# First k cast, V and W1 casts, and the order of batch 1's loads in a fused attention and MLP kernel

## The chip, the cores and the metric

The kernel runs on one core of one Trainium2 chip. The metric is the time on the device in microseconds, lower is better. The core's engines run side by side and meet at semaphores: TensorE (PE) multiplies matrices and transposes, VectorE (DVE), ScalarE (ACT) and GpSimd (POOL) work element by element, and SyncE (SP) issues most of the transfers (DMAs).

## The reference

Eight batches of 576 tokens with 8 heads of 64. Attention sees a window of 64 tokens; its output goes through a normalisation and a two-layer MLP with a residual.

```python
scores = scale * np.matmul(q, k.transpose(0, 1, 3, 2))
mask = (rel >= 0) & (rel < window)                       # window = 64
attn = softmax(np.where(mask, scores, -1000000000.0))
x = np.matmul(attn, v)                                   # heads side by side: [8, 576, 512]
xn = (x - mu) / np.sqrt(var + 1e-06) * g_ln
out = x + np.maximum(xn @ w_ch1, 0.0) @ w_ch2            # [512, 2048], [2048, 512]
```

## The kernel before

Inputs and weights are float32 in memory and are cast to float16 on the chip. The work is cut into nine groups: group b (0 to 7) is the first 512 tokens of batch b, and group 8 the last 64 tokens of all batches. A group has four blocks of 128 tokens. One block goes through these steps:

- `t_main` (from L268) transposes q or k of half a group on TensorE and copies the result from PSUM to `qkT`. Groups 0 to 2 use it.
- `s_mm` (L302) multiplies k by q and lets ScalarE take the exponential into `pt`; `s_mask` multiplies by the mask on VectorE. In group 0 the mask is added on TensorE.
- `b_step` (L369) multiplies `pt` by V. It needs V twice: in `vA` as it is, and in `vB` shifted by 64 tokens. For group 0 and half of group 1, `vB_cur` and `vB_prev` (L194, L197) fill `vB` from the float32 V, on the engine that is given by a number: 0 is ScalarE, 1 is VectorE. VectorE then divides by the sums (L387, L390) and takes mean and variance (L392, L394).
- `z_step` (L406) normalises to `z`, `zt_step` (L447) transposes `z` to `zT`.

The MLP of a group follows: the first layer (L512, and L549 for half a group at a time) multiplies `w1g` by `zT` and ScalarE takes the maximum with zero (L516, L554); the second layer multiplies the result `hrT` by `w2s`. In group 0 the second layer is `l2_three` (L557), whose matmuls are at L563: three blocks of tokens side by side, staggered by one step, so that the step (i, 0) is the first that reads W2 tile i, which is 256 rows of W2. The last block of tokens follows in `l2` (L525). From group 2 on the second layer is a scheme of seven products (L590).

W1 comes in eight tiles (`w1_load`, i = 0 to 7): column quarter i // 2, and rows i % 2. The first four lie in a pool of four buffers, the last four in the memory that `w2s` takes later. `w1_cast(i, c, engine, lo, hi)` (L232) scales by the normalisation's gain and casts half of a tile's rows. W2 comes in eight tiles through the same pool of four buffers (`w2_load`, L242), so that tile i + 4 can only be loaded once GpSimd has cast tile i (`w2_cast`, L249).

The order of the work is written by hand. The instructions of an engine run in the order in which the program names them. What comes ahead of the loop is a list of calls (from L647). In the loop each group's matmuls are cut into units, and `at(u, f, ...)` puts the call f behind unit u. SyncE's queue is the order of the load calls: q, k and v of batch 0, the eight tiles of W1, q and k of the first half of batch 1 (`load_qk(1, 0)`), and the first four tiles of W2. The rest stands in `rest_of_loads` (L731), which is called behind unit 7 of group 0 and gives both SyncE's and GpSimd's order for batch 1. `keep_clock` issues matmuls whose result isn't used.

Of the kernel before, what the change touches and what calls it, by code (L numbers as in the profile page):

```python
# [11 lines left out]
FP16 = mybir.dt.float16  # L12
# [6 lines left out]
def kernel(  # L19
# [10 lines left out]
    nc = tc.nc  # L30
# [118 lines left out]
    def cast_q(b, x, half, act=False):  # L149
        t = qk32.pop((b, x, half))  # L150
        dst = p_in.tile([128, 8, 2, D], FP16, tag=f"qk16_{x}", name=f"qk16_{x}_{b}_{half}")
        qk16[(b, x, half)] = dst
        j = 8 if b < NPE else 2 if x == 1 else 4
        cp(act, dst[:, :].rearrange("p (a j) e d -> p a e j d", j=j),
           t[:, :].rearrange("p (a e j d) -> p a e j d", e=2, j=j, d=D))

    def alloc_v(b):
        vA[b] = p_va.tile([128, 4, H, D + 1], FP16, tag="vA", name=f"vA_{b}")
        nc.gpsimd.memset(vA[b][:, :, :, D:D + 1], 1.0)
# [18 lines left out]
    def cast_v(b, c0, c1, act=False):  # L178
        cp(act, vA[b][:, c0:c1, :, 0:D], v32[b][:, c0:c1])
# [9 lines left out]
    def init_vB(b):  # L189
        alloc_vB(b)  # L190
        nc.gpsimd.memset(vB[b][:, :, :, D:D + 1], 1.0)
        nc.gpsimd.memset(vB[b][0:64, 0, :, D:D + 1], 0.0)
# [59 lines left out]
    def alloc_qkT(b):  # L252
        qkT[b] = [p_qkt.tile([128, NHP, SM + 64 * x], FP16, tag=f"qkT{x}", name=f"qkT{x}_{b}") for x in range(2)]
        if b >= NPE:
            nc.gpsimd.memset(k_runs(b)[:, :, 0:32], 0.0)
        else:
            nc.gpsimd.memset(qkT[b][1][:, :, 0:64], 0.0)
# [4 lines left out]
    def evac(x, out, in_):  # L262
        if x == 0:
            nc.scalar.copy(out=out, in_=in_)
        else:
            nc.vector.tensor_copy(out=out, in_=in_)

# [397 lines left out]
    )  # L665
    nc.vector.tensor_scalar(out=mbias, in0=mask, scalar1=-1.0, scalar2=30000.0, op0=ALU.add, op1=ALU.mult)
    alloc_qkT(0)
    cast_q(0, 0, 0)
    alloc_v(0)
    cast_q(0, 1, 0)  # L670
    init_vB(0)
    cast_v(0, 0, 1)
    cast_v(0, 1, 2)
    cast_qk(0, 1)
    cast_v(0, 2, 3)
    cast_v(0, 3, 4)
    w1_cast(0, 0, nc.gpsimd)
    w1_cast(1, 0, nc.gpsimd, 0, 256)
    w1_cast(1, 0, nc.gpsimd, 256, 512)
    for i, lo in ((2, 0), (3, 0), (2, 256)):  # L680
        w1_cast(i, 0, nc.gpsimd, lo, lo + 256)

    for f in (alloc_qkT, alloc_v, init_vB):
        f(1)

    def keep_clock(n, pool=ps_t, tag="tp"):
        warm = pool.tile([128, 512], FP32, tag=tag, name="warm")
# [6 lines left out]
    keep_clock(9, ps_mm, "mm")  # L694
    t_main(0, 0, 0, 0)
    keep_clock(1, ps_mm, "mm")
    t_main(0, 1, 0, 1)
    keep_clock(1, ps_mm, "mm")
    vB_cur(0, 0, 0)
    vB_cur(0, 1, 0)  # L700
    vB_prev(0, 0, 1)
    vB_prev(0, 1, 1)
    s_mm(0, 0, True)
    s_mm(0, 1, True, (ps_mm, "mm"))
# [8 lines left out]
    vB_cur(0, 2, 0)  # L713
    keep_clock(2, ps_mm, "mm")
    s_mm(0, 2, True)
    vB_cur(0, 3, 1)
    vB_prev(0, 2, 1)
    keep_clock(1)
    zt_step(0, 1)
    w1_cast(0, 1, nc.scalar)  # L720
    b_step(0, 2)
    z_step(0, 2)
    w1_cast(1, 1, nc.scalar)
# [3 lines left out]
    load_qk(1, 0)  # L727
    for i in range(4):
        w2_load(i)

    def rest_of_loads():  # L731
        cast_qk(1, 0)
        for i in range(8):
            w2_cast(i)
            if i < 4:
                w2_load(i + 4)
        load_v(1, 0, 2)
        cast_v(1, 0, 1)
        cast_v(1, 1, 2)
        load_qk(1, 1)  # L740
        load_v(1, 2, 4)
        cast_qk(1, 1)
        cast_v(1, 2, 3)
        cast_v(1, 3, 4)
        load_qk(2, 0)
        load_qk(2, 1)

    def tail_casts(i, act, *us):
        return tuple((u, cast_tail, i, part, act) for part, u in enumerate(us))
# [12 lines left out]
    for g in range(NGRP):  # L762
# [33 lines left out]
        if g == 0:  # L796
            at(0, b_step, 0, 3)
            at(0, z_step, 0, 3)
            at(0, w1_cast, 2, 1, nc.scalar)
            at(0, w1_cast, 3, 1, nc.scalar)  # L800
            at(0, w1_cast, 3, 0, nc.scalar, 256, 512)
            at(1, zt_step, 0, 2)
            at(2, zt_step, 0, 3)
            for j in range(4):
                at(3 + j, w1_cast, 4 + j, 0, nc.vector)
                at(3 + j, w1_cast, 4 + j, 1, nc.gpsimd if j % 2 else nc.scalar)
                at(10 + j, r_step, 0, j)
            at(7, rest_of_loads)
            at(11, t_main, 1, 0, 0, 1)
            at(12, t_main, 1, 1, 0, 1)  # L810
            at(17, s_mm, 1, 0)
            at(19, s_mask, 1, 0)
            at(20, s_mm, 1, 1)
            at(22, s_mask, 1, 1)
            at(30, vB_cur, 1, 0, 0)
            at(30, vB_prev, 1, 0, 1)
            at(32, vB_cur, 1, 1, 0)
            at(33, vB_prev, 1, 1, 0)
            at(33, b_step, 1, 0)
            at(35, r_step, 1, 0)  # L820
            at(35, z_step, 1, 0)
            at(36, b_step, 1, 1)
            at(38, r_step, 1, 1)
            at(38, z_step, 1, 1)
            at(41, zt_step, 1, 0)
            at(42, zt_step, 1, 1)
            at(43, t_main, 1, 0, 1, 0)
            at(44, load_v, 2, 0, 4)
            at(26, keep_k, 0)
            at(27, lambda: nc.gpsimd.memset(vt8[:, :, :, :, D:D + 1], 1.0))  # L830
            at(27, keep_v, 0)
            at(28, alloc_qkT, 2)
            at(28, cast_q, 2, 0, 0)
            at(29, cast_q, 2, 1, 0)
            at(29, make_vB_half, 1)
            at(41, lambda: pace(zT[1][:, 0, 0:1]))
            at(41, cast_q, 2, 0, 1)
            at(43, cast_q, 2, 1, 1)
        if g == 1:
            at(2, t_main, 1, 1, 1, 1)  # L840
            at(4, s_mm, 1, 2)
            at(5, s_mask, 1, 2)
            at(6, s_mm, 1, 3)
            at(7, s_mask, 1, 3)
            at(7, b_step, 1, 2)
            at(7, t_main, 2, 0, 0, 0)
            at(8, t_main, 2, 1, 0, 0)
            at(9, b_step, 1, 3)
            at(10, t_main, 2, 0, 1, 0)
            at(10, r_step, 1, 2)  # L850
            at(10, z_step, 1, 2)
            at(11, t_main, 2, 1, 1, 0)
            at(12, zt_step, 1, 2)
            at(12, r_step, 1, 3)
            at(12, z_step, 1, 3)
            at(14, zt_step, 1, 3)
            at(4, alloc_v, 2)
            at(4, alloc_vB, 2)
            for c in range(4):
                at(5 + c, cast_v, 2, c, c + 1)  # L860
            at(8, make_vB, 2)
            at(9, keep_k, 1)
            at(9, keep_v, 1)
            at(9, keep_v, 2)
            at(20, keep_k, 2)
            at(10, late_masks, 2)
            for j in range(4):
                at((13, 16, 19, 22)[j], s_mm, 2, j)
                at((14, 17, 20, 23)[j], s_mask, 2, j)
                bz((16, 19, 22, 25)[j], 2, j)  # L870
                at((20, 23, 26, 29)[j], zt_step, 2, j)
        if g > 0:
            if g == 1:
                for u, i, c in ((12, 1, 0), (13, 1, 1), (14, 2, 0), (15, 2, 1)):
# [30 lines left out]
        if 0 < g and b + 1 < B:  # L905
            n = b + 1
            e = 3 if g == 1 else 1
            at(e, load_qk, n, 0)
            at(e + 1, load_qk, n, 1)
            at(e + 4, load_v, n, 0, 4)  # L910
            if g == 1:
                at(10, alloc_qkT, n)
                for j, (x, half) in enumerate(((0, 0), (1, 0), (0, 1), (1, 1))):
                    u = (16, 19, 22, 27)[j]
                    at(u, (lambda: pace(zsd[(b, 3)][:, 0:1])) if j == 3 else lambda j=j: pace(rcps[(b, j)][:, 0:1]))
                    at(u, cast_q, n, x, half)
                at(20, x_main, n, 0)
                at(27, x_main, n, 1)
                at(12, alloc_v, n)
                at(12, alloc_vB, n)  # L920
                for u, c, j in ((21, 0, 0), (22, 1, 0), (24, 2, 1), (24, 3, 1)):
                    if c < 3:
                        at(u, (lambda j=j: pace(zT[b][:, 0, 128 * j:128 * j + 1])) if c % 2 == 0 else
                           (lambda j=j: pace(rss[(b, j)])))
                    at(u, cast_v, n, c, c + 1)
                at(24, make_vB, n)
                at(26, keep_v, n)
            else:
                at(6, keep_k, b)
                at(3, alloc_qkT, n)  # L930
                at(16, alloc_v, n)
                at(16, alloc_vB, n)
                for u, x, half in ((16, 0, 0), (16, 1, 0), (17, 0, 1), (18, 1, 1)):
                    at(u, cast_q, n, x, half, True)
                at(17, x_main, n, 0)
                at(19, x_main, n, 1)
                for c in range(4):
                    at((18, 20, 20, 21)[c], cast_v, n, c, c + 1, True)
                at(22, make_vB, n)
                at(22, keep_v, n)  # L940
# [37 lines left out]
```

## Time and profile before

| | |
|---|---|
| median of 3 runs | 303.81 us (303.74 to 304.11) |
| the profiled execution, its own time | 304.84 us |
| its span, by the profile | 303.0 us |
| TensorE busy | 289.7 us (96%) |
| VectorE, ScalarE busy | 194.8 us (64%), 189.9 us (63%) |
| GpSimd busy | 108.8 us (36%) |
| read from HBM, written | 36.70 MB, 9.44 MB |

The span runs from the first to the last instruction of the profiled execution; its own time has 1.84 us more around it. All times inside the kernel are microseconds from the start of the span. A row of a timeline gives start and length, the engine and line, the operation with what it writes and reads, how many instructions are merged in it, and in brackets how long the engine was idle before and what ended that. "PEld" is the loading of weights into TensorE, which lies beside its matmuls; "SPq" is SyncE issuing DMAs.

### The profile page before, as it was taken

The page shows a single profiled execution, that of the slowest core. Times are in us where ns is not written, and L with a number is a line of the kernel's source. Part 1 is how long each engine was busy: PE and PEld are TensorE (multiplying, and loading weights), DVE is VectorE, ACT ScalarE, POOL GpSimd, SP SyncE. Part 2 cuts the span into 40 slices and gives each one's busy share as a digit, 9 for nine tenths or more (in the row PEclk, how much of TensorE's full clock was granted, in tenths as well). Part 3 has the DMA queues.
Part 4 walks back from the last instruction along what each step waited for, and adds up shares of the span by engine and source line. Part 5 has one row for each costly group of instructions (what it writes and reads, how often), then busy time and mean ns, then how long its engine had stood idle before and what let it go on. Part 6 is the DMA issues. An engine that isn't in the chain of part 4 may idle for free.

```text
span 303.0 us, 7956 instructions
## 1 busy us (share of the span) xinstructions
PE 289.7 (96%) x3259; PEld 187.1 (62%) x3259; DVE 194.8 (64%) x353; ACT 189.9 (63%) x372; POOL 108.8 (36%) x194
## 2 busy tenths in 40 slices
PE   5788999999999999999999999999999999999993
PEld 2456544765854478547855784578457845884582
DVE  0696317457984997389638954895489877641362
ACT  3598733576856894589368937892785978307500
POOL 3778775997786203400440043004171010000000
PEclk9799999999999999999999999999999999999999
DMA  6999799999957969997999899899967930003005
GB/s 186 279 368 386 252 272 276 278 303 279 219 115 209 259 127 168 298 247 128 189 319 228 105 200 322 196 118 204 276 123 153 158 141 0 2 21 117 2 0 138
DMA packets 108371, 58.03 MB, mean 192 GB/s; under 512 B 82240, under 2 KB 98112, under 8 KB 108336
## 3 DMA queue, kind: packets, MB, share of 16 engines
q1 hardware_dynamic: 103696, 45.50, 67.1%
q0 software_dynamic: 3680, 11.52, 12.6%
q10 hardware_dynamic: 960, 0.53, 0.6%
q8 instruction: 25, 0.41, 0.6%
q14 instruction: 10, 0.08, 0.1%
HBM read 36.70 MB, written 9.44 MB: 152 GB/s over the span
## 4 chain that ended last, share of the span: by engine, by line
PE 75%; DMA 11%; SPq 5%; POOL 3%; ACT 2%; DVE 2%; issue 1%; POOLq 0%
PE hps L512 33%; PE wX L590 16%; PE wZ L590 8%; PE wY L590 4%; DMA v<-in_v_dram 4%; PE xps L383 4%; SPq L83 3%; DMA w2s<-in_moe_w_ch_dram 3%; PE sc L326 2%; PE ch L525 2%; DMA vt<-vA 2%; SPq L173 2%; PE hph L549 2%; DMA qk<-in_k_dram 1%; PE ztp L453 1%; PE sc L333 1%
## 5 line engine op out<-in xcount | busy, mean ns | idle before, releaser
L512 PE MATMUL hps<-zT,w1g 128*128 128x512 f16 x480 | 109.7, 379 | 0.0
L516 ACT ACTIVATE hrT<-hps 128x512 f16<-128x512 f32 x120 | 71.3, 596 | 54.0 <-PE hps L512 52.8
L512 PEld LDWEIGHTS <-w1g 128*128 128x128 f16 x480 | 44.8, 98 | 49.5
L590 PEld LDWEIGHTS <-sw 128*128 128x128 f16 x448 | 43.5, 98 | 5.0
L590 PEld LDWEIGHTS <-hrT 128*128 128x128 f16 x336 | 32.4, 98 | 5.4
L367 DVE TENSOR_TENSOR pt<-pt,mask 128x1024 f16<-128x1024 f16 x28 | 20.0, 713 | 20.9 <-ACT pt L347 12.6
L207 POOL DMA_DIRECT2D vB<-vA x10 | 5.1, 518 | 77.9 <-ACT vA L145 77.6
L472 POOL DMA_DIRECT2D out_dram<-osb x20 | 13.2, 660 | 54.4 <-DVE osb L608 50.1
L392 DVE BATCH_NORM_STATS2 stats<-xn 128x6 f32<-128x512 f32 x36 | 25.0, 695 | 1.2
L390 DVE TENSOR_TENSOR xn<-xps,rcp 128x512 f32<-128x512 f32 x36 | 24.9, 691 | 1.2
L347 ACT ACTIVATE pt<-sc 128x512 f16<-128x512 f32 x40 | 23.7, 594 | 2.5 <-PE sc L326 2.5
L501 DVE TENSOR_TENSOR sw<-hrT 128x1024 f16<-128x1024 f16 x28 | 19.0, 678 | 9.7 <-ACT hrT L516 9.7
L549 PE MATMUL hph<-zT,w1g 128*128 128x256 f16 x192 | 23.7, 273 | 0.4 <-POOL w1g L240 0.2
L414 DVE TENSOR_SCALAR z<-xn,mv,rs 128x512 f16<-128x512 f32 x32 | 19.8, 617 | 5.0 <-ACT rs L404 4.5
L608 DVE TENSOR_TENSOR osb<-wX,xn 128x512 f32<-128x512 f32 (+1 forms) x24 | 14.9, 621 | 9.9 <-PE wX L590 9.9
L353 ACT ACTIVATE pt<-sc 128x512 f16<-128x512 f32 x32 | 17.6, 594 | 5.0 <-PE sc L333 4.6
L147 POOL CAST qk<-qk 128x1024 f16<-128x1024 f32 x16 | 17.1, 1076 | 9.0 <-DMA qk<-in_q_dram 6.0
L549 PEld LDWEIGHTS <-w1g 128*128 128x128 f16 x192 | 17.9, 98 | 3.5 <-POOL w1g L240 0.5
L383 PEld LDWEIGHTS <-pt 128*64 128x64 f16 x576 | 12.1, 110 | 12.8 <-issue 8.5
L525 PE MATMUL ch<-w2s,hrT 128*128 128x512 f16 x80 | 19.8, 379 | 0.0
L456 ACT COPY zT<-ztp 128x512 f16<-128x512 f16 x21 | 12.3, 584 | 9.6 <-PE ztp L453 9.5
L554 ACT ACTIVATE hrT<-hph 128x512 f16<-128x512 f32 x24 | 14.2, 598 | 3.4 <-PE hph L549 3.2
(108 smaller groups left out, 439.3 us busy)
## 6 DMA issues: line engine op xcount, KB each, us to landing
w2s<-in_moe_w_ch_dram SPq DMA_DIRECT2D x12, 512.0 KB, 9.4
out_dram<-osb POOLq DMA_DIRECT2D x12, 512.0 KB, 7.0
qk<-in_q_dram SPq DMA_DIRECT2D x10, 512.0 KB, 7.7
qk<-in_k_dram SPq DMA_DIRECT2D x10, 512.0 KB, 9.5
v<-in_v_dram SPq DMA_DIRECT2D x40, 128.0 KB, 5.9
qk<-in_q_dram SPq DMA_DIRECT2D x12, 256.0 KB, 5.0
qk<-in_k_dram SPq DMA_DIRECT2D x12, 256.0 KB, 4.8
v<-in_v_dram SPq DMA_DIRECT2D x12, 256.0 KB, 5.7
```

The lines of the kernel that those rows point to most:

```text
L347: nc.scalar.activation(out=pt[:, par].rearrange("k h w (p j) -> k (h w) p j", j=4), in_=sc[:, :].rearrange("k h w (j p) -> k (h w) p j", j=4),
L367: nc.vector.tensor_tensor(out=ptv, in0=ptv, in1=mb, op=ALU.mult)
L383: nc.tensor.matmul(out=xps[64 * r:64 * r + 64, h, :D + 1], lhsT=pt[:, par, hp, r, :], rhs=rhs, start=True, stop=True)
L390: nc.vector.tensor_tensor(out=xn, in0=xps[:, :, 0:D], in1=rcp_b, op=ALU.mult)
L392: nc.vector.bn_stats(out=stats, in_=xn.rearrange("p h d -> p (h d)"))
L414: nc.vector.tensor_scalar(out=z, in0=x, scalar1=mv[:, 0:1], scalar2=rss[(g, kb)][:, 0:1], op0=ALU.subtract, op1=ALU.mult)
L501: nc.vector.tensor_tensor(out=S[i], in0=a, in1=b, op=op)
L512: nc.tensor.matmul(out=hps, lhsT=w1g[:, kc, 128 * hc:128 * (hc + 1)], rhs=zT[g][:, kc, :], start=(kc == KCS[0]), stop=(kc == KCS[-1]),)
L516: nc.scalar.activation(out=hrT[:, hc, :], in_=hps, func=AF.Relu, bias=0.0, scale=1.0)
L525: nc.tensor.matmul(out=ch[kb], lhsT=hrT[:, hc, 128 * kb:128 * (kb + 1)], rhs=w2s[:, hc, :], start=(hc == 0), stop=(hc == NHC - 1),)
L549: nc.tensor.matmul(out=hps[:, e], lhsT=w1g[:, kc, 128 * hc:128 * (hc + 1)], rhs=zT[g][:, kc, 256 * half:256 * half + 256], start=(kc == KC ...
L590: nc.tensor.matmul(out=xyz[bank][t * two_banks][:, t], lhsT=lhsT, rhs=rhs, start=bool(first and (t == 0 or two_banks) and hc == 0), stop=( ...
```

## The change

A function `cast_k0` is added that casts the first half of batch 0's k on VectorE, in two instructions, one for each of the two DMAs that bring it. The copy of its transposes goes from VectorE to ScalarE. Four V copies of batch 0 move: blocks 0 and 1 of `vB_cur` from ScalarE to VectorE, block 3 of `vB_cur` and block 2 of `vB_prev` from VectorE to GpSimd, for which `evac` knows the number 2. W1 casts: (0, 1) goes from ScalarE to VectorE, and (1, 0), which was two GpSimd instructions, becomes one on VectorE. The memsets for batch 1 (`alloc_qkT`, `alloc_v`, `init_vB`) are issued ahead of batch 0's casts. In SyncE's queue batch 1's v, and its q and k of the second half, are issued behind W2 tile 3 and ahead of W2 tile 4; GpSimd's casts of them are named between those of the W2 tiles. Last, some steps of batches 1 and 2 are put one unit later or exchanged.

```diff
+    def cast_k0():
+        t = qk32.pop((0, 1, 0))
+        dst = p_in.tile([128, 8, 2, D], FP16, tag="qk16_1", name="qk16_1_0_0")
+        qk16[(0, 1, 0)] = dst
+        for e in range(2):
+            nc.vector.tensor_copy(out=dst[:, :, e], in_=t[:, 512 * e:512 * e + 512].rearrange("p (j d) -> p j d", d=D))
...
         if x == 0:
             nc.scalar.copy(out=out, in_=in_)
+        elif x == 2:
+            nc.gpsimd.tensor_copy(out=out, in_=in_)
...
     alloc_qkT(0)
+    alloc_qkT(1)
+    alloc_v(0)
+    alloc_v(1)
     cast_q(0, 0, 0)
-    alloc_v(0)
-    cast_q(0, 1, 0)
     init_vB(0)
+    init_vB(1)
+    cast_k0()
     cast_v(0, 0, 1)
     cast_v(0, 1, 2)
     cast_qk(0, 1)
     cast_v(0, 2, 3)
     cast_v(0, 3, 4)
+    vB_prev(0, 2, 2)
+    vB_cur(0, 3, 2)
     w1_cast(0, 0, nc.gpsimd)
-    w1_cast(1, 0, nc.gpsimd, 0, 256)
-    w1_cast(1, 0, nc.gpsimd, 256, 512)
...
-    for f in (alloc_qkT, alloc_v, init_vB):
-        f(1)
...
-    t_main(0, 1, 0, 1)
+    t_main(0, 1, 0, 0)
     keep_clock(1, ps_mm, "mm")
-    vB_cur(0, 0, 0)
-    vB_cur(0, 1, 0)
+    vB_cur(0, 0, 1)
     vB_prev(0, 0, 1)
+    vB_cur(0, 1, 1)
     vB_prev(0, 1, 1)
...
     s_mm(0, 2, True)
-    vB_cur(0, 3, 1)
-    vB_prev(0, 2, 1)
+    w1_cast(0, 1, nc.vector)
     keep_clock(1)
     zt_step(0, 1)
-    w1_cast(0, 1, nc.scalar)
+    w1_cast(1, 0, nc.vector)
...
     for i in range(4):
         w2_load(i)
+    load_v(1, 0, 2)
+    load_qk(1, 1)
+    load_v(1, 2, 4)
 
     def rest_of_loads():
         cast_qk(1, 0)
...
             w2_cast(i)
             if i < 4:
                 w2_load(i + 4)
-        load_v(1, 0, 2)
-        cast_v(1, 0, 1)
-        cast_v(1, 1, 2)
-        load_qk(1, 1)
-        load_v(1, 2, 4)
-        cast_qk(1, 1)
+            if i == 3:
+                load_qk(2, 0)
+                cast_v(1, 0, 1)
+                cast_v(1, 1, 2)
+            if i == 5:
+                cast_qk(1, 1)
+                load_qk(2, 1)
         cast_v(1, 2, 3)
         cast_v(1, 3, 4)
-        load_qk(2, 0)
-        load_qk(2, 1)
...
-            at(42, zt_step, 1, 1)
-            at(43, t_main, 1, 0, 1, 0)
-            at(44, load_v, 2, 0, 4)
+            at(42, t_main, 1, 0, 1, 0)
+            at(43, zt_step, 1, 1)
+            at(40, load_v, 2, 0, 4)
...
-                bz((16, 19, 22, 25)[j], 2, j)
-                at((20, 23, 26, 29)[j], zt_step, 2, j)
+                bz((16, 20, 23, 25)[j], 2, j)
+                at((20, 24, 27, 29)[j], zt_step, 2, j)
...
-                    u = (16, 19, 22, 27)[j]
+                    u = (16, 20, 23, 27)[j]
```

## The prediction

> **What bounds the kernel now.** First the page: how busy each engine is, and where in the span it is not.
>
> ```profile
> PE 289.7 (96%) x3259; PEld 187.1 (62%) x3259; DVE 194.8 (64%) x353; ACT 189.9 (63%) x372; POOL 108.8 (36%) x194
> PE   5788999999999999999999999999999999999993
> GB/s 186 279 368 386 252 272 276 278 303 279 219 115 209 259 127 168 298 247 128 189 319 228 105 200 322 196 118 204 276 123 153 158 141 0 2 21 117 2 0 138
> ```
>
> A slice is 7.6 us. TensorE is full from the fourth slice on, so time can be won only in the first 26 us, but it can be lost anywhere. The waits of TensorE up to 75 us say how much is left to win:
>
> ```profile
> PE tp L272 <- POOL qk L147: 1.8, 1, 1.8
> PE ztp L453 <- DVE z L412: 1.7, 2, 1.1
> PE ztp L453 <- DVE z L414: 0.6, 2, 0.5
> ```
>
> (Engine, line, releaser, us in total, times, longest.) The first row is the wait for GpSimd's cast of the first k, the second ends with the transposes of the last z of batch 0, the third is one late z of batch 1. TensorE's timeline gives the places:
>
> ```profile
> 25.41 0.40 PE L453 MATMUL ztp<-ident,z 128*128 128x128 f16 x4 [1.10 <-DVE z L412]
> ...
> 41.09 5.79 PE L563 MATMUL ch<-w2s,hrT 128*128 128x512 f16 x26
> ...
> 47.18 1.47 PE L563 MATMUL ch<-w2s,hrT 128*128 128x512 f16 x6
> ...
> 53.72 0.40 PE L453 MATMUL ztp<-ident,z 128*128 128x128 f16 x4 [0.49 <-DVE z L414]
> ```
>
> After 25.41 no wait exceeds 0.5 us. The L563 rows are batch 0's second layer, which eats the W2 tiles in order. From 41.09 to the next row (46.80) 26 matmuls take 0.2196 us each. Each unit of `l2_three` has two matmuls, and the unit (i, 0) is the first to read W2 tile i; counted out, tile 4 is first read 8 matmuls in (42.85), tile 5 at 44.16, tile 6 at 45.48, and tile 7 opens the row at 47.18. Now GpSimd's timeline, which shows when each tile is ready, and SyncE's, which issues the loads:
>
> ```profile
> 37.30 1.04 POOL L250 CAST w2s<-w2s 128x1024 f16<-128x1024 f32 x1 [0.33 <-DMA w2s<-in_moe_w_ch_dram]
> 38.63 1.04 POOL L250 CAST w2s<-w2s 128x1024 f16<-128x1024 f32 x1 [0.29 <-DMA w2s<-in_moe_w_ch_dram]
> 40.59 1.56 POOL L250 CAST w2s<-w2s 128x1024 f16<-128x1024 f32 x1 [0.92 <-ACT pt L353]
> 42.73 1.17 POOL L250 CAST w2s<-w2s 128x1024 f16<-128x1024 f32 x1 [0.57 <-DMA w2s<-in_moe_w_ch_dram]
> 44.36 1.04 POOL L250 CAST w2s<-w2s 128x1024 f16<-128x1024 f32 x1 [0.46 <-DMA w2s<-in_moe_w_ch_dram]
> ...
> 52.77 0.62 POOL L147 CAST vA<-v 128x512 f16<-128x512 f32 x1 [0.41 <-DMA v<-in_v_dram]
> ```
> ```profile
> 23.73 15.00 SPq L245 DMA_DIRECT2D w2s<-in_moe_w_ch_dram  x8
> 38.79 1.18 SPq L173 DMA_DIRECT2D v<-in_v_dram  x2
> 40.01 4.71 SPq L83 DMA_DIRECT2D qk<-in_q_dram  x2
> ```
>
> The first POOL row is W2 tile 3, the next four tiles 4 to 7, ready at 39.67, 42.15, 43.90 and 45.40: only 1.6 to 3.2 us ahead of their first use. The last is batch 1's last V piece. **So the second layer of batch 0 runs on W2 tiles that come just in time from a transfer-bound start.** The table of 2 us windows shows the transfers' one hole:
>
> ```profile
> 30.00:32.00 2.00, 2.00 (x13) 1.03 (x11) 0.00 (x0) 1.35 (x3) 1.13 (x2) 1.00 1.04 386
> 34.00:36.00 2.00, 2.00 (x20) 1.24 (x18) 1.61 (x2) 1.68 (x7) 1.42 (x3) 1.00 0.38 105
> ```
>
> (Last columns: clock, DMA share, GB/s.)
>
> **What the Trainium skill says.** "DMA: Bandwidth & Descriptors", section "Queues, rings and completion order": on each DMA engine descriptors are taken in the order of the ring, and all loads of one issuing engine share one row of rings. The trace agrees for these loads: casts that wait for them start in the order of issue. So what SyncE issues ahead of a W2 tile delays it by its whole transfer. The same page, "Specifications", asks for pieces of at least 512 B for full rate; V comes in rows of 64 floats (256 B), and its two pieces of 256 KB are cast 45.42 and 46.45, 1.03 us apart, against 1.33 us for 512 KB of W2 (37.30 to 38.63): slower per byte, as said. "TensorE: Matmul & The Clock Gate", section "Why this matters for your kernels": an idle gap of about 3 us drops the clock to half. Windows of before have one such stretch, granted clock 0.50 from 9 to 12 us, after the 1.83 us wait for k.
>
> **Part 1, the start.** `cast_k0` replaces one GpSimd cast (1.04 us, 7.46 to 8.50) by two VectorE casts of 128x512. No row of before has this form; the W1 cast on VectorE is nearest (0.47 to 0.90 us). The first half lands earlier, so about 0.5 us of it follows the landing at 7.4: TensorE's k transposes start near 7.9, not 8.56. Their copy moves from VectorE (1.23) to ScalarE (1.01), idle since `vB_cur` left it. Together about 0.9 us for the first scores. V copies: two ScalarE ones (0.62 each) go to VectorE (0.43 to 1.26), two VectorE ones to GpSimd (nearest row 0.62), which is idle until the first W1 tile (16.87). W1: GpSimd loses two casts (about 2 us), VectorE gains two of about 0.5. They stand between z 1 and the third reciprocal, which waited on VectorE's two V copies (1.32) until 19.44 and now wait for W1 tile 1; that had landed by ScalarE's cast at 19.14-20.47, so a delay there is at most about 0.5 us. The memsets for batch 1 move from 24.16-25.9, where they lie beside the 1.58 us z (others 0.49), into GpSimd's idle 2.24-4.79 and before the first V cast; there they may lie beside the new k cast, which could stretch it by as much (1.1), so this part's lower bound is a small loss. SyncE's load of k (1, 0) now waits for VectorE's cast in place of GpSimd's; both end before 9, the load is issued at 21.02: nothing. Floor: W1 tile 3 starts its cast at 22.39 for lack of data, and TensorE's first-layer block 4 waits for it until 23.37; loads ahead of that are unchanged. So what can be won is the 1.10 wait at 25.41 and little else: -0.3 to 1.3 us, I take 1.2.
>
> **Part 2, the loads.** SyncE now issues batch 1's v 0-1, q and k of half 1, v 2-3 (eight DMAs, 2 MB) between W2 tiles 3 and 4. All four W2 tiles 4-7 move behind them. Fed one behind the other, V pieces cost 1.03 each, q and k 0.66 (casts at 30.59 and 31.91, two DMAs apart): 4 x 1.03 + 4 x 0.66 = 6.8 us. As measured after tile 7, with SyncE's 4.07 us issue of one q behind two V's, 8.4 (44.36 to 52.77). Tile 3 has landed at 37.2, so the last V lands between 44.0 and 45.6; I take 44.7, since the hole shown above is filled. Then 1.35 per tile: tile 4 at 46.05, 5 at 47.4, 6 at 48.75, 7 at 50.1.
> GpSimd casts in the written order: tile 4 done 47.15, tile 5 48.5, then q and k of half 1 (2 x 1.07, whose data came earlier, but which now stand ahead), 50.65, tile 6 51.7, tile 7 52.75.
> TensorE in order: tile 4 at 47.15 against 42.85 (4.3 late), tile 5 4.35, tile 6 51.7 against 45.48 (6.2 late); the six matmuls and b_step to tile 7 take 1.7, so it isn't waited for. **TensorE stands 6.2 us later from there on**, and part 1's 1.2 is inside it: arriving early only lengthens the wait. Queued behind the waiting matmul: batch 1's b_steps, z transposes, and everything after; nothing of theirs is late for another reason, so all of it shifts along.
>
> **Part 3, moves in batch 1 and 2.** Batch 1's v, q, k stop being late, but TensorE waited at most 0.5 for anything of theirs. Transposes of z 1 go behind q's: their wait (0.49) ends, but ScalarE must then do q's copy (1.01) and zT's (0.59) before the next matmul, with 0.86 + 0.23 of TensorE work beside them: about 0.7 of waiting, net +0.2. Batch 2's b_steps a unit later: TensorE shows no wait named there, so 0; bounds -0.3 and +0.5. Loads of batch 2 follow where GpSimd ends near 53.4, as before; TensorE being later, they are covered.
>
> Sum: +6.2 +0.2 +0 = +6.4. The profiled execution's span is 303.0 and its own time 304.84; they would become 309.4 and 311.2. It lies 1.03 above the median 303.81; against that, **310.2**.
>
> **Rivals.**
> - *Transfers alone decide* (0.22): the k and q casts don't hold tile 6, or the ring drains faster. Then tile 5's 4.35 stands: 308.4. For: tile 6 lands 3 us before its cast. Against: GpSimd is in order.
> - *Slower ring and half clock* (0.14): W1's four tiles behind two V's took 14.96 to 22.39, 7.4 and not 5.4. Tile 5 then lands near 49.2, tile 6 is cast by 53.5: 8.0 late; if the 5 us idle halves the clock, six matmuls add 1.3: 312 to 313.2.
> - *Faster* (0.04): the hole swallows the loads. Windows of 5 us show 270 and 243 GB/s from 30 and 35; against 386 that leaves (116 + 143) x 5, room for 1.3 MB of the 2 MB; for no wait tile 4 must be cast by 41.65 and tile 6 by 44.3. Then part 1 stays: 303.8 - 1.2 - 0.2 = 302.4.
> - *Nothing* (0.03): wait and gain cancel, 303.8.
>
> The main case has 0.57. Range: 307.2 to 313.0, from transfers alone less 1 to the slow ring. A measurement here tells about 0.2% (0.6 us). Slower 0.93, same 0.03, faster 0.04.
>
> **What would show it.** In the changed profile: a TensorE wait of 4 to 6 us at L572 (L563 of before) released by GpSimd's W2 cast, from about 41.7; a second of about 2 before tile 6; W2 tile 4's cast starting near 46; k transposes near 7.9; no z wait of 1.1 near 25; perhaps a clock digit under 9 near 47. Wrong if W2 casts 4 to 7 start before 42.

## The result and the profile after

| kernel | median of its runs, us | runs | ratio to before, 95% interval |
|---|---|---|---|
| before | 303.77 | 303.65 to 304.11 | |
| after | 313.99 | 313.88 to 314.05 | 1.0334 [1.0316, 1.0352] |

The change costs 10.2 us. The profiled execution of after has a span of 312.3 us and an own time of 314.05, which lies on its median; that of before lay 1.07 above its own. The two profiles therefore differ by only 9.3 us of span.

First the page of after: busy times, TensorE's row of 40 slices (7.8 us each), and its granted clock.

```profile
PE 290.9 (93%) x3259; PEld 187.3 (60%) x3259; DVE 196.3 (63%) x356; ACT 189.2 (61%) x370; POOL 106.7 (34%) x193
PE   5879928899999999999999999999999999999993
PEclk9999987999999999999999999999999999999998
```

A "2" stands in TensorE's sixth slice (39 to 47 us), an "8" in the seventh and eighth, and the clock has a dent in the sixth and seventh. Everything from the ninth slice on is full, as before. The waits of TensorE up to 95 us (engine, line, releaser; us in total, times, longest) give the names:

```profile
PE ch L572 <- POOL w2s L257: 6.7, 2, 6.5
...
PE tp L281 <- ACT zT L465: 1.4, 1, 1.4
...
PE hph L558 <- ACT zT L465: 0.7, 1, 0.7
```

In the part that is read here, lines of after are 9 higher than before's from L272 on, and 7 higher between L161 and L262: L572 is the L563 of before, L257 its L250. TensorE's timeline gives the places (start, length):

```profile
47.76 4.13 PE L572 MATMUL ch<-w2s,hrT 128*128 128x512 f16 x12 [6.54 <-POOL w2s L257]
52.06 1.45 PE L572 MATMUL ch<-w2s,hrT 128*128 128x512 f16 x6 [0.17 <-POOL w2s L257]
...
61.28 0.61 PE L281 MATMUL tp<-ident,qk 128*128 128x128 f16 x8 [1.40 <-ACT zT L465]
...
63.65 2.78 PE L558 MATMUL hph<-zT,w1g 128*128 128x256 f16 x24 [0.67 <-ACT zT L465]
```

The first row is the wait for W2 tile 4, as forecast. The second wait, before tile 6, is 0.17 and not 2: the 12 matmuls between them took 0.34 us each on the mean (4.13 / 12), against 0.22 in before. The windows show the clock at half (the third last number of a line is the granted clock):

```profile
42.00:44.00 2.00, 0.00 (x0) 0.00 (x0) 0.00 (x0) 0.31 (x1) 0.00 (x0) 0.94 1.03 361
44.00:46.00 2.00, 0.00 (x0) 0.00 (x0) 0.00 (x0) 0.00 (x0) 0.00 (x0) 0.50 0.83 231
...
48.00:50.00 2.00, 2.00 (x6) 0.75 (x5) 0.00 (x0) 0.00 (x0) 1.99 (x3) 0.50 1.05 403
50.00:52.00 2.00, 1.89 (x8) 0.64 (x7) 0.00 (x0) 0.00 (x0) 2.00 (x4) 0.85 0.68 210
```

GpSimd's timeline, tile by tile: tile 4, tile 5, the k and q casts of batch 1 that now stand ahead, tiles 6 and 7, and, five microseconds later, the first q and k of batch 2:

```profile
46.67 1.04 POOL L257 CAST w2s<-w2s 128x1024 f16<-128x1024 f32 x1 [8.61 <-DMA w2s<-in_moe_w_ch_dram]
48.01 1.04 POOL L257 CAST w2s<-w2s 128x1024 f16<-128x1024 f32 x1 [0.30 <-DMA w2s<-in_moe_w_ch_dram]
48.99 2.03 POOL L147 CAST qk<-qk 128x1024 f16<-128x1024 f32 x2
50.96 2.03 POOL L257 CAST w2s<-w2s 128x1024 f16<-128x1024 f32 x2
...
56.08 2.03 POOL L147 CAST qk<-qk 128x1024 f16<-128x1024 f32 x2
```

The last row is the part that the prediction did not see. On VectorE at that moment is z of block 0 of batch 1. In before it stood at 49.76, well ahead of these casts, and took 0.77 us (before's two rows first, then after's):

```profile
49.76 0.77 DVE L414 TENSOR_SCALAR z<-xn,mv,rs 128x512 f16<-128x512 f32 x1
```
```profile
55.54 2.03 POOL L147 CAST qk<-qk 128x1024 f16<-128x1024 f32 x2
```
```profile
56.41 1.99 DVE L423 TENSOR_SCALAR z<-xn,mv,rs 128x512 f16<-128x512 f32 x1
...
60.79 0.55 DVE L423 TENSOR_SCALAR z<-xn,mv,rs 128x512 f16<-128x512 f32 x1
```

That it matters is told by the chain of work that ended last (start, us, what), in which this z is one link, and ScalarE's zT copy a later one, straight ahead of the q transposes:

```profile
52.06 1.45 PE ch L572 x6
...
56.41 1.99 DVE z L423
...
60.75 0.48 ACT zT L465
...
61.28 0.61 PE tp L281 x8
```

**One measure for all runs.** To place a loss, TensorE's lateness against the first profile of before is read at four points: matmuls with the same tiles are paired in order, and the median of the differences of their starts within 1.5 us of the point is taken. For example, the first-layer row of 24 matmuls of batch 1 starts at 63.65 in after and at 55.27 in before, so after is there 8.4 late. "Start" is read near 33 us, ahead of the first late tile, and "first layer of batch 1" at the end of that layer, near 64 us.

| run | start | after W2 tile 6 | first layer of batch 1 | after batch 1 (94 us) |
|---|---|---|---|---|
| before again (e0) | -0.59 | -0.59 | -0.79 | -0.69 |
| after | -1.76 | +6.65 | +8.36 | +9.31 |
| e1, loads back | +0.43 | +0.43 | +2.06 | +2.87 |
| e2, loads only | -0.95 | +6.66 | +7.44 | +7.49 |
| e3, start only | -1.23 | -1.23 | -1.66 | -1.72 |
| e4, k and q casts behind | -1.08 | +5.73 | +8.39 | +9.35 |
| e5, clock kept | -0.99 | +6.57 | +8.26 | +9.22 |
| e6, both | -0.52 | +5.20 | +5.93 | +6.55 |
| e7, batch 2's casts later | -1.02 | +6.22 | +7.07 | +8.03 |
| e8, swap back | +0.88 | +6.17 | +7.19 | +8.14 |
| e9, units back | -1.29 | +7.67 | +8.12 | +8.19 |
| e10, two V ahead | -1.39 | -0.44 | +0.97 | +0.70 |
| e11, q and k ahead | -0.95 | -0.62 | +0.92 | +0.64 |
| e12, e11 and casts later | -1.83 | -1.30 | -0.20 | -0.47 |
| e13, six loads, casts later | -0.48 | +5.08 | +5.11 | +4.83 |

The first profile of before had a late start: seven executions with before's start stand at 0 to -1.83 (mean -0.88), nine with the changed start at +0.88 to -1.76 (mean -0.73).

### The profile page after: what moved, and what is told of

It reads as the page before. It is cut to its first block, busy times and chain, and to the rows that moved or that the text cites. A ratio compares the mean times of both kernels' runs of the same rounds, so it can differ in the third digit from the quotient of the medians.

```text
span 312.3 us, 7958 instructions
## 1 busy us (share of the span) xinstructions
PE 290.9 (93%) x3259; PEld 187.3 (60%) x3259; DVE 196.3 (63%) x356; ACT 189.2 (61%) x370; POOL 106.7 (34%) x193
## 4 chain that ended last, share of the span: by engine, by line
PE 74%; SPq 8%; DMA 7%; DVE 5%; issue 2%; ACT 1%; POOL 1%; DVEq 0%
PE hps L521 32%; PE wX L599 16%; PE wZ L599 8%; DMA qk<-in_q_dram 5%; PE wY L599 4%; SPq L83 4%; PE xps L392 4%; PE ch L534 3%; PE hph L558 3%; PE sc L335 2%; SPq L180 2%; DMA w1s<-in_moe_w_ch_dram 2%; SPq L252 1%; DVE stats L401 1%; DVE xn L399 1%
## 5 line engine op out<-in xcount | busy, mean ns | idle before, releaser
L412 ACT ACTIVATE rs<-mv,epst 128x1 f32<-128x1 f32 x36 | 10.8, 299 | 22.8 <-DVE mv L403 22.7
L396 DVE RECIPROCAL rcp<-xps 128x8 f32<-128x8 f32 x36 | 7.3, 202 | 25.3 <-PE xps L392 25.3
L534 PE MATMUL ch<-w2s,hrT 128*128 128x512 f16 x80 | 19.9, 380 | 0.0
L572 PE MATMUL ch<-w2s,hrT 128*128 128x512 f16 x48 | 12.9, 414 | 6.7 <-POOL w2s L257 6.7
```

What stands on the lines that cost most here:

```text
L534: nc.tensor.matmul(out=ch[kb], lhsT=hrT[:, hc, 128 * kb:128 * (kb + 1)], rhs=w2s[:, hc, :], start=(hc == 0), stop=(hc == NHC - 1),)
```

## The experiments

Ratios are to before, measured on the same chip at the same time. Three chips were used. Times scattered more there than in the table of the result: on two of them before itself ranged over some 8 us. Effects of 1 us are therefore read from the table above, which has one profiled execution of each kernel, rather than from the medians.

**The change taken apart: e0 to e3.** e0 is the kernel before, unchanged.

> The kernel before, unchanged, profiled a second time. The first profiled execution took 304.84 us, 1.07 above the median of the timed runs (303.77), while that of the changed kernel (314.05) lies on its median (313.99). Theory A: the first profile caught a slow start of about 1 us (first-layer W1 tile 3 landed at 22.3 there, at 21.6 in the changed kernel, though nothing stands ahead of it in either); then this profile's own time is about 303.8, its span about 302, and W1 tile 3's cast on GpSimd starts near 21.6. Theory B: profiling always costs this kernel 1 us; then about 304.8 and 22.4 again.

Measured: 304.28 us, 1.0003 [0.998, 1.0027]. The profiled execution took 304.17, so the times are those of theory A. Its cause is not: the cast of W1 tile 3 starts at 22.84, later than in the first profile (22.39). What is gone is the wait of 1.10 for z near 25 us.

e1 is the changed kernel with its loads in the old order, e2 the kernel before with only the new order of loads and their casts, e3 the kernel before with only the changed start (W1 casts, V copies, `cast_k0`). In e1 and e2 the body of `rest_of_loads` and the unit of batch 2's V load go with the loads:

```
     for i in range(4):
         w2_load(i)
+    load_v(1, 0, 2)        # e2; e1 takes these three lines out of the changed kernel
+    load_qk(1, 1)
+    load_v(1, 2, 4)
```

> The changed kernel with the order of batch 1's loads and casts as before; the start and the unit moves of batches 1 and 2 stay changed. Theory 'loads': the whole loss is the late W2 tiles and what follows from TensorE's shift; about 302 to 303.5 us (the start's gain of 0.8 to 1.8 less up to 1 for the unit moves), no TensorE wait for a W2 cast. Rival 'unit moves': the 1.7 us at the start of batch 1's first layer and the 0.95 us behind it come from the exchanged and postponed steps; then these stay, 303.8 - 1.2 + 2.6 = about 305.

Measured: 305.58, 1.0049 [1.0024, 1.0074].

> The kernel before with nothing but batch 1's loads and casts in the changed order. Theory 'loads': W2 tiles 4 to 7 land when the transfers are through, whatever TensorE did before, so the start's gain is irrelevant: 311 to 313 us, with one TensorE wait of about 5 us for a W2 cast near 43 to 48. Rival 'unit moves': 309 to 310.5, as the boundary of batch 1 and its second half then run as before.

Measured: 312.87, 1.0301 [1.0275, 1.0327].

> The kernel before with the changed start alone (k cast on VectorE, V copies and W1 casts exchanged, memsets early). Theory 'gain at the start': the wait of 1.1 us for the last z of batch 0 goes, 302.3 to 303.0 us. Rival 'noise': TensorE's 1.77 us lead in the changed kernel came mostly from transfers that were late in the first profile of before; then 303.4 to 303.9.

Measured: 303.63, 0.9989 [0.9962, 1.0016].

So the loads are 3.0% of the 3.3%, the start is nothing that can be told, and what is in e1 and not in e3, the swap and the later units of batch 2, is about 0.6%. The timeline of e2 shows the wait, and that here the 18 matmuls of tiles 4 to 6 took 0.33 us each on the mean, against 0.22 in before:

```profile
47.55 5.97 PE L563 MATMUL ch<-w2s,hrT 128*128 128x512 f16 x18 [5.52 <-POOL w2s L250]
```

**What sets tile 6: e4, e5, e6.** Two things could hold TensorE between tile 4 and tile 6: its half clock, and GpSimd's two casts ahead of tile 6. (e4's expectation reckons with 0.43 us for each of the 12 matmuls; the mean was 0.34, since the clock came back before the last of them.) e4 removes the second, e5 the first, e6 both.

```
e4:  -            if i == 5:          # casts of q and k of half 1
     +            if i == 7:
e5:  +            at(24, keep_clock, 26, ps_s, "sc")   # ahead of the first unit of tile 4
```

> The changed kernel, with GpSimd's k and q casts of batch 1's second half behind W2 tiles 6 and 7, not ahead of them. Theory A (the half clock, not GpSimd's order, sets TensorE's place after the wait): the 12 matmuls of tiles 4 and 5 still take 0.43 us each, so tile 6 is reached no earlier than about 51.9; at most 0.3 us gained, 313.7 to 314.0. Rival B (GpSimd's order holds tile 6, as the prediction had it): tile 6's cast ends about 2 us earlier and TensorE gains 1.5 us, 312.5.

Measured: 314.05, 1.0337 [1.0263, 1.041].

> The changed kernel, with 26 added matmuls (keep_clock, about 5.7 us at full clock, results not used) on TensorE in the wait for W2 tile 4, so that the clock stays full. Theory A (half clock and GpSimd's order cover each other): tiles 4 and 5 are eaten in 2.6 us, but tile 6 is then waited for until about 52.0, with a second TensorE wait of about 1.5 to 2 us; at most 0.3 us gained, 313.7 to 314.0. Rival C (the half clock alone cost the time): 1.5 us or more gained, 312.5 or less.

Measured: 314.6, 1.0335 [1.0274, 1.0395].

> The changed kernel with both edits: k and q casts behind tiles 6 and 7, and 26 added matmuls in the wait. Theory A: only with both gone does TensorE reach tile 6 earlier, near 50.4 (tile 6 lands about 49.2, cast 1.04), a gain of 1.3 to 1.8 us, 312.2 to 312.7, while each edit alone gives at most 0.3. Rival B or C: as much as the better of the two single edits. Rival D (nothing but the last landing counts): no gain from any of the three.

Measured: 311.47, 1.0227 [1.0168, 1.0286].

The three timelines of TensorE, in this order; in e4 the 18 matmuls of tiles 4 to 6 run without a wait but slowly, in e5 the fast ones wait 1.50 for tile 6, in e6 18 matmuls go through at full speed:

```profile
47.06 5.54 PE L572 MATMUL ch<-w2s,hrT 128*128 128x512 f16 x18 [5.16 <-POOL w2s L257]
```
```profile
41.83 5.78 PE L700 MATMUL warm<-mbias,ident 128*128 128x512 f16 x26
47.70 2.79 PE L572 MATMUL ch<-w2s,hrT 128*128 128x512 f16 x12
51.98 1.46 PE L572 MATMUL ch<-w2s,hrT 128*128 128x512 f16 x6 [1.50 <-DMA qk<-in_k_dram]
```
```profile
47.92 4.14 PE L572 MATMUL ch<-w2s,hrT 128*128 128x512 f16 x18
```

The releaser in e5 is named as the k load; what came last on the way is GpSimd, whose timeline has the k and q casts at 48.92 to 50.94 and tiles 6 and 7 behind them from 50.89, as in after. Tile 4 came at a different time in each execution, so each is reckoned from its own. Against before's 42.85 TensorE reached tile 4 late by 4.91 (after), 4.21 (e4), 4.85 (e5) and 5.07 (e6); after tile 6 it was late by 6.65, 5.73, 6.57 and 5.20. Between the two it lost 1.74, 1.52, 1.72 and 0.13. Theory A holds for this stretch: two covers lie over each other, and removing either one alone gains 0.2 us or nothing.

e4 also stood 0.9 us earlier than after behind tile 6, of which 0.7 is its earlier tile 4. None of it reached the first layer (+8.39 against +8.36), because the z of the boundary took it back: begun earlier, it took 2.94, and ended at 58.43 as against 58.40 in after.

```profile
55.49 2.94 DVE L423 TENSOR_SCALAR z<-xn,mv,rs 128x512 f16<-128x512 f32 x1
```

So e4's unchanged time alone would not have shown the cover. e6 gains another microsecond at the batch boundary, which no theory had: there TensorE comes earlier still against GpSimd's casts of batch 2 (56.99), and its z, at 54.96, took 1.01.

**The boundary: e7 and e8.** e7 moves GpSimd's first two casts of batch 2 behind zT of batch 1; e8 puts the transposes of z 1 back ahead of q's.

```
e7:  -            at(28, cast_q, 2, 0, 0)
     -            at(29, cast_q, 2, 1, 0)
     +            at(41, cast_q, 2, 0, 0); at(41, cast_q, 2, 1, 0)   # behind the pace() at 41
e8:  +            at(42, zt_step, 1, 1)
     +            at(43, t_main, 1, 0, 1, 0)     # the two lines of after removed
```

> The changed kernel, with GpSimd's casts of batch 2's first q and k (2 x 1.02 us from 56.08) moved behind zT of batch 1, so that they no longer lie beside VectorE's z of block 0 of batch 1. Theory (the two engines get in each other's way): that z takes about 0.55 us instead of 1.99, TensorE's wait of 1.40 at the q transposes goes or falls under 0.3, and the time falls by 0.8 to 1.4 us, to 312.6 to 313.2. Rival (z is slow for another reason, or the swapped order of z and q transposes alone makes the wait): no change, within 0.3 us of 314.0.

Measured: 313.91, 1.0322 [1.0245, 1.0399].

> The changed kernel with the transposes of z 1 of batch 1 put back ahead of those of the second q. Theory (the swap costs, since q's copy then stands ahead of zT's copy on ScalarE): the first layer of batch 1 starts without the 0.67 wait, 0.6 to 1.1 us less than the changed kernel's 314.0, 312.9 to 313.4. Rival (the prediction's +0.2): no difference that can be told, 313.8.

Measured: 313.58, 1.0314 [1.0271, 1.0358].

Neither median can tell 0.9 us from nothing; the places can. From tile 6 to batch 1's first layer after loses 8.36 - 6.65 = 1.71, e7 0.85, e8 1.02. (e8's execution lost 2.5 us more near 162, in a wait for a DMA of a late batch; of the other runs only e12 shows such a wait.) VectorE and TensorE of e7:

```profile
55.98 1.13 DVE L423 TENSOR_SCALAR z<-xn,mv,rs 128x512 f16<-128x512 f32 x1
```
```profile
59.99 0.61 PE L281 MATMUL tp<-ident,qk 128*128 128x128 f16 x8 [0.54 <-ACT zT L465]
...
62.35 2.78 PE L558 MATMUL hph<-zT,w1g 128*128 128x256 f16 x24 [0.67 <-ACT zT L465]
```

With the casts gone z is faster, though not the 0.55 expected: GpSimd's copies into vB moved up beside it (55.78 to 56.82). The q transposes wait 0.54 and not 1.40. This wait goes with the length of z: 1.40 with a z of 1.99, 0.54 with 1.13, 0.42 with 1.01 (e6), and none over 0.2 with 0.73 (e9, below). The 0.67 ahead of the first layer is in all of them, and is the swap's own. e9 has the swap with hardly any collision, since its TensorE came a microsecond later, and loses 8.12 - 7.67 = 0.45 there. Both waits come about on ScalarE, whose queue in after reads:

```profile
60.22 0.30 ACT L412 ACTIVATE rs<-mv,epst 128x1 f32<-128x1 f32 x1 [3.85 <-DVE mv L403]
...
60.66 0.57 ACT L465 COPY zT<-ztp 128x512 f16<-128x512 f16 x1
61.92 1.01 ACT L271 COPY qkT<-tp 128x1024 f16<-128x1024 f16 x1 [0.69 <-PE tp L281]
```

The zT copy of block 0 stands behind the rs of block 1, which waits for block 1's statistics. The q transposes need no z at all, yet by the profile they are released by that copy. Put ahead of z 1 they wait for nearly what z 1 waits for, and then q's copy (1.01) stands ahead of the last zT copy. In e8, without the swap, the whole 1.50 us is one wait of z 1's transposes for z, and there is no wait at the first layer.

**Batch 2's units: e9.**

```
e9:  -  bz((16, 20, 23, 25)[j], 2, j);  zt_step at (20, 24, 27, 29);  casts at (16, 20, 23, 27)
     +  bz((16, 19, 22, 25)[j], 2, j);  zt_step at (20, 23, 26, 29);  casts at (16, 19, 22, 27)
```

> The changed kernel with batch 2's b_steps, z transposes and casts put back to the units of the kernel before. Theory (batch 2's steps a unit later cost what was lost between the start of batch 1 and 96 us): TensorE's place after batch 1 is 0.5 to 1.0 us earlier, 313.0 to 313.5, and the wait of 0.5 at xps for VectorE's mask is gone. Rival (the prediction's 0; the loss has another source, the later batch 2 data): no difference, 314.0.

Measured: 312.92, 1.0295 [1.0252, 1.0339]. Waits of TensorE from 76 to 100 us, after and then e9:

```profile
PE xps L392 <- DVE pt L376: 0.5, 1, 0.5
PE hph L558 <- ACT hrT L563: 0.3, 1, 0.3
```
```profile
PE xps L392 <- DVE pt L376: 0.2, 1, 0.2
```

The table is clearer than any wait: from the first layer of batch 1 to 94 us every run with the later units loses 0.62 to 0.96 (after, e1, e4 to e8), every run with the old ones -0.28 to +0.10 (e0, e2, e3, e9 to e13). The later units cost about 0.9; the named waits make up 0.6 of it, and the rest was not traced further.

**How many loads are too many: e10, e11, and then e12, e13.** e10 is before with only the first two V pieces ahead (0.5 MB), e11 with only q and k (1 MB).

```
e10: + load_v(1, 0, 2)     e11: + load_qk(1, 1)     # behind the first four w2_load
e13: + both                e12, e13: also e7's edit (batch 2's casts later)
```

> The kernel before, with only the first two V pieces of batch 1 (0.5 MB, 2.1 us of transfer) issued between W2 tiles 3 and 4. Theory (each load ahead delays the tiles by its whole transfer, less the 0.7 us by which tile 4 was early): TensorE waits about 1.4 us for tile 4, total 1.0 to 1.8 us over before, 304.8 to 305.6. Rival (the hole in the transfers at 34 to 36 us holds 0.5 MB): at most 0.3 us over before, 303.8 to 304.1.

Measured: 305.57, 1.0059 [1.0037, 1.008].

> The kernel before, with only q and k of batch 1's second half (1 MB, 2.6 us of transfer) issued between W2 tiles 3 and 4, their casts where they were. Theory (whole transfer, less 0.7 us): TensorE waits 1.9 us for tile 4, total 1.5 to 2.3 us over before, 305.3 to 306.1; with the other run it makes a straight line to the 9 us of all eight loads only if SyncE's slow issue behind V adds its own share. Rival (the hole takes up to 1.3 MB): at most 0.3 us over before.

Measured: 306.13, 1.0074 [1.0051, 1.0096].

The times fit the theory, and the profiles refute it. e11 has no wait for W2 at all, and e10 one of 0.3. Waits of TensorE from 38 to 60 us in e11, and its SyncE:

```profile
PE ztp L453 <- DVE z L414: 2.0, 1, 2.0
```
```profile
28.50 1.21 SPq L83 DMA_DIRECT2D qk<-in_q_dram  x2
29.84 1.21 SPq L83 DMA_DIRECT2D qk<-in_k_dram  x2
33.05 4.43 SPq L245 DMA_DIRECT2D w2s<-in_moe_w_ch_dram  x4
```

The q and k loads are issued by 31.1; W2 tile 4 is issued at 33.05, when GpSimd has cast tile 0 and so freed one of the four staging buffers. In before, SyncE stood idle there, from 28.2 to 34.3, between W2 tiles 3 and 4 (and its waits up to 36 us have one of 5.0 for W2):

```profile
23.73 4.42 SPq L245 DMA_DIRECT2D w2s<-in_moe_w_ch_dram  x4
```
```profile
34.34 4.39 SPq L245 DMA_DIRECT2D w2s<-in_moe_w_ch_dram  x4
```
```profile
SPq L245 <- DMA w2s<-in_moe_w_ch_dram: 7.6, 4, 5.0
```

So 1 MB goes into time in which nothing could be issued. TensorE still lost 0.95 (e10) and 0.33 (e11) up to tile 6, of which the W2 tiles are 0.3 and nothing; most of the rest lies in batch 1's first use of V. The 2.0 us are again z of batch 1 beside GpSimd's casts of batch 2, which came earlier because batch 1's data did:

```profile
52.27 2.03 POOL L147 CAST qk<-qk 128x1024 f16<-128x1024 f32 x2
```
```profile
52.22 2.37 DVE L414 TENSOR_SCALAR z<-xn,mv,rs 128x512 f16<-128x512 f32 x1
```

> The kernel before with q and k of batch 1's second half (1 MB) issued between W2 tiles 3 and 4, and GpSimd's first two casts of batch 2 moved behind zT of batch 1. Theory (SyncE stood idle from 28.2 to 34.3 us before W2 tile 4 for want of a staging buffer, so 1 MB ahead is free, and the 2.0 us that the same loads cost without the moved casts were VectorE's z beside GpSimd's casts): no z over 1.2 us, no wait of TensorE over 0.6 us near 54, and the time is before's, within 0.4 us. Rival (the loads themselves cost it): 1.5 to 2.3 us over before, as without the moved casts.

Measured: 305.37, 1.0029 [1.0, 1.0058]. With the casts away, z took 0.83 and 0.55, and batch 1's first layer starts 1.44 early, after 1.30 early behind tile 6: the boundary costs nothing. The collision came back later in that layer. TensorE waits 1.2 for VectorE's mask, which takes 0.71 on the mean in before and here stood beside GpSimd's four V casts of batch 2:

```profile
60.46 2.98 DVE L367 TENSOR_TENSOR pt<-pt,mask 128x1024 f16<-128x1024 f16 x1 [2.13 <-ACT pt L353]
```
```profile
60.62 2.28 POOL L147 CAST vA<-v 128x512 f16<-128x512 f32 x4
```

The W2 tiles cost nothing again. The time lies 0.3% over before with an interval that reaches down to 1.0, so "before's, within 0.4 us" is neither met nor excluded. (The profiled execution lost 4.9 us after 180 us, where TensorE waits 3.0 for a DMA; only what lies ahead is used.)

> As the run with q and k ahead and the casts later, with the first two V pieces ahead too (six loads, 1.5 MB). Theory (idle time of SyncE first, then every load counts): the eight loads end SyncE's issue at about 38.5 and tile 4 landed 8 us later than before; two V pieces less end it near 37, so tile 4 lands near 43 to 44.5 and is cast by 44 to 45.5 against a first use near 42: TensorE waits 2 to 3.5 us and the time is 2 to 4 us over before. Rival (in proportion to the bytes: 0.75 of 8.4): 6 us over before. Rival (1.5 MB still fits): within 0.5 us of before.

Measured: 309.75, 1.0171 [1.0139, 1.0202].

```profile
46.22 5.73 PE L563 MATMUL ch<-w2s,hrT 128*128 128x512 f16 x18 [3.71 <-POOL w2s L250]
```

With 1.5 MB the wait is back, 3.7 us, and the half clock adds about 1.8 (18 matmuls in 5.73): +5.56 from the start to tile 6. That is over the 2 to 4 expected, because the clock was not in the sum. The boundary costs nothing (+0.03), z having been kept clear. From the start to tile 6 TensorE loses 0.3 to 1.0 at 0.5 and 1 MB (e10 to e12), 5.6 at 1.5 MB and 7.6 at 2 MB (e2): a threshold, and no proportion.

Bytes are not all of it. The q loads behind two V's block SyncE itself while they are issued, which e11's expectation had left open. In e13 they take 4.15 us (1.21 in e11, where no V stands ahead), and SyncE comes to W2 tile 4 only at 38.70, against 32.96 in e10, 33.05 in e11 and 34.34 in before. In after it is the same:

```profile
31.51 4.16 SPq L83 DMA_DIRECT2D qk<-in_q_dram  x2
...
38.62 4.81 SPq L252 DMA_DIRECT2D w2s<-in_moe_w_ch_dram  x4
```

Tile 4's cast starts 8.0 us later in after than in before (46.67 and 38.63); 4.3 of it is the later issue, and the rest is the longer time from issue to cast (8.0 against 4.3). How much of either V's short rows make was not separated: no run has 1 MB of V ahead, or 1.5 MB without V.

No version beat both kernels: e3 is before's time within its interval, e12's interval just reaches it, and the others are slower.

## Why the prediction was off

The forecast was slower by 6.4 us, 310.2; the kernel takes 313.99, above the range's end of 313.0. Its main mechanism, the late W2 tiles, was right and nearly right in size. The step that failed is the sentence "so all of it shifts along", with the two terms behind it in Part 3: they were put at +0.2 and 0, and measured +1.71 and +0.95. The difference of 3.8 us has four parts, each a term of the sum.

- **The loads (6.2 late at tile 6): right in place and mechanism, 0.45 short.** Tile 4's cast started at 46.67 (forecast: landing at 46.05), tile 6's place is 52.06 (forecast 51.7). Also right: an earlier start only lengthens the wait; starts from +0.88 to -1.76 came out at +6.17 to +6.66 in five runs (after, e2, e5, e7, e8). e4, whose tile 4 came 0.7 earlier than after's, came out at +5.73, and e9, where the half clock covered nearly all of tiles 4 to 6, at +7.67. Two details inside the term were wrong and cancelled. The second wait of 2 us turned into slow matmuls, and the half clock, kept for a rival with 1.3 us, was there; e4 to e6 show that clock and cast order cover each other. And "what SyncE issues ahead of a W2 tile delays it by its whole transfer" is not true of the first megabyte (e10, e11). The rival "faster" reckoned with a hole of 1.3 MB; the runs put the limit between 1 and 1.5 MB, and 2 MB were moved. (Its 302.4 also takes Part 3's loss of 0.2 for a gain.)
- **The start: 1.2 us of gain, placed inside the wait; nothing measured.** e3 gives 0.9989 [0.9962, 1.0016]. The 1.10 wait for z near 25 us belonged to one execution: none of the six other runs with the same start shows it, and they stand 0.5 to 1.8 us earlier near 33. From the same source came an error of the baseline. The forecast carried over the 1.03 us by which before's profile lay above its median; after's profile lies on its median. That is 1.0 us of the 3.8.
- **Batch 1's swap (+0.2): it measured +1.7 with its collision, 1.5 short.** The wait of 0.7 for zT was foreseen and is there (0.67). Not foreseen were the wait of the q transposes for the zT copy, and that a TensorE six microseconds later puts z of batch 1 beside GpSimd's casts of batch 2. GpSimd's queue did not shift along by the same amount. Its casts moved from 55.54 to 56.08, and the z of before, at 49.76, to 56.41. e7 shows the collision at 0.9, e8 what the swap adds to it, about 0.7. Without most of the collision the swap measured 0.45 (e9), not far from the forecast, so the missed collision is the larger part.
- **Batch 2's units (0, bounds -0.3 and +0.5): +0.95, outside its own bounds.** That TensorE showed no wait there only said that the steps were in time as they stood, not that they had room for a unit. e9 takes 0.9 of it back, and every run of the table agrees.

0.45 + 1.0 + 1.5 + 0.95 is 3.9, against 3.8 measured.

## What to carry to other kernels

Before pricing a load that is issued ahead of another, ask when the later one could have been issued at all: here it waited for a staging buffer, so one megabyte ahead of it made TensorE wait at most 0.3 us for a weight tile, while 1.5 and 2 MB came with a stall and a half clock. When a change delays one engine, list what the others do at the new time, not only what waits for it: an engine that does not shift along can meet an instruction that it never met before. Reckon a gain in front of such a meeting with care: an engine that comes earlier may only wait longer, as in e4. And take two profiles of the kernel before when terms of one microsecond matter; a wait seen in one execution may not be there in the next.

## What the runs showed of the hardware

**VectorE's z is held until GpSimd's casts are done.** The z of 128x512 to 16 bits takes 0.55 us alone. In e11 it started at 52.22 and ended at 54.59, beside two casts that ended at 54.30; in e4 it took 2.94. In eight runs (after, e2, e4, e5, e8 to e11) it ended 0.28 or 0.29 us behind the end of the second cast, wherever it had begun. The mask of e12 (2.98 us) likewise ended 0.5 behind the last of four casts. The Trainium skill, "SBUF — State Buffer", section "Who interferes with whom", says that VectorE in its two-port modes and GpSimd share a pair of ports, which whoever issues first holds for a whole instruction, while the other blocks. That fits, though no trace shows whether z ran in such a mode, and with one thing more: z did not get in between the two casts, but waited for both. That is not so everywhere. In before the z at 52.92 ended at 53.67, 0.28 behind a V cast, and it was GpSimd's next copy that took 0.59 in place of 0.40.

**The half clock came in stretches of 3.4 us, and the length of a wait does not settle whether it comes.** In e8 TensorE waited 2.54 us for tile 4, and its windows show the clock falling after the work had begun again:

```profile
46.00:48.00 2.00, 1.59 (x5) 0.65 (x5) 0.00 (x0) 0.00 (x0) 0.81 (x2) 0.68 1.00 351
...
50.00:52.00 2.00, 1.25 (x6) 0.45 (x5) 0.00 (x0) 0.00 (x0) 2.00 (x3) 0.96 0.99 354
```

A mean of 0.68 over 2 us is 1.28 us at half, so the clock fell at 46.7; 0.96 puts its return at 50.2, 3.4 us later. In after 0.94 and 0.85 in the windows further up put the fall at 43.8, some 2.5 us into a wait of 6.5, and the return at 50.6: 6.8 us, twice as long. Shorter waits went both ways. After those of 1.83 in before and 2.34 in e0, both near 8 us, the clock fell; after those of 2.03 in e11 and 1.90 in e10, near 54 us, it stayed at 1.00. The gap of about 3 us that the prediction cites was not needed. "TensorE: Matmul & The Clock Gate", section "What's actually happening", says that activity is judged in windows of 3413 ns that run freely and do not start anew with a kernel. The stretches have that length, and the different places of the fall agree with it.
